# Turning k and q of the second chunk with half-array matmuls in place of quarter ones

## Chip, cores and metric

The kernel runs on one core of a Trainium2 chip. The metric is the device time of one execution in microseconds (us); less is better. All times in this document are in us unless marked ns. The engines of the core have short names: PE is TensorE (its weight loads are listed as PEld), ACT is ScalarE, DVE is VectorE, POOL is GpSimd and SP is SyncE, which issues DMAs.

## What is computed

Attention with a sliding window of 128 positions and 4 sink positions over 4 batches, 8 heads, 768 positions and a head size of 64, followed by a layer norm and an MLP (512 to 2048 to 512) with a residual. Cut to what matters:

```python
scores = scale * np.matmul(q, k.transpose(0, 1, 3, 2))
keep = is_sink | in_window            # pos < 4, or 0 <= i - j < 128
scores = np.where(keep, scores, -1000000000.0)
a = np.exp(scores - max); a = a / (sum + 1e-09)
x = np.matmul(a, v)                   # heads side by side: [4, 768, 512]
xn = (x - mu) / np.sqrt(var + 1e-06) * g_ln
out = x + np.maximum(xn @ w_ch1, 0.0) @ w_ch2
```

## The kernel before

The 3072 rows are worked in 24 tiles of 128 rows; two tiles make a chunk of 256 rows, three chunks a batch. A chunk is loaded, its k and q are turned (transposed, so that the head size lies on the partitions), each of its tiles goes through scores, exponential, masking and the product with v, is centred and transposed (`xnt`), and then the chunk goes through the MLP: eight groups `ph` that write the hidden layer, and after them eight groups `pc` for the output.

Everything is entered as an operation `P.op(name, engines with costs, priority, emit, reads, writes, ...)` in a planner (`Plan`). `Plan.run` places the operations on the engines in simulated time, takes buffers and PSUM banks from rings, picks ACT or DVE where either can do it, and so fixes the order of each engine's program by hand. The `mode` of a PE operation names the tiling of the array (`"q"` quarters, `"c"` column quarters, `"n"` the whole array, `"r"` row halves); where the mode changes the planner adds 0.095. Behind the plan, filler matmuls (L1133) that write an unused bank are put where the plan leaves PE idle for more than 0.3 in the first 24 us.

k and q are turned in three ways. Chunk 0 is cast and turned by whole-array matmuls (L667). Chunks 1, 2 and 3 go through `by_pairs`: one load brings 256 rows as [128 partitions, 8 heads, 2, 64], so that partition p holds the rows 2p and 2p+1 (index i), and matmuls against the identity turn them. From chunk 4 on the DMA engines do it (L691 and L572).

For chunk 1 `by_pairs` is called once for k and once for q (L678), with two PSUM banks of the ring `one` each; for chunks 2 and 3 it is called once for both, with one pair of banks per tensor from the ring `pair`. The turn of a tensor (`tr`, L588) is 32 matmuls (L595), each with 64 rows by 64 columns of the array: 4 head pairs, 2 values of i, 2 heads of the pair (columns of the array) and 2 halves of the partitions (rows, index r). Half r of the partitions holds the rows of tile 2c+r, and its results go to bank r. So each of the two evictions of a tensor (`evict`, L604, run at L638) copies one bank, which is one tile's 128 positions for all head pairs, into `T[:, :, 128 r ...]`. `tile_of[name, tile, half of the heads]` records which eviction a tile's operations have to wait for; here it is the tile's own eviction for both halves of the heads.

`attend_tile` (L723) takes tiles 0 to 3. Its scores run as two operations, j = 0 and 1, with two head pairs each (L748, matmuls L759 for tiles 0 and 1 and L718 in `bands` for tiles 2 and 3); operation j waits for `need[j]` (L728), which is made of `tile_of` entries. For tiles 0 to 2 mask matmuls (`pm`, L739) fill the bank first. `sk` (L771, matmuls L773) makes the scores of the sinks for all head pairs of a tile. `value` (L827) multiplies with v (L840, L845), takes the reciprocal of the sum (L858), scales (L860); `normalise` (L865) takes the statistics (L868, L870), subtracts the mean (L872), and PE transposes the result (L885), which DVE evicts with the gain (L896). The first chunk's MLP groups use L1026, 16 matmuls each; the later chunks use L1033, and the output groups L1062. L1043 and L1045 are the evictions of a `ph` group on ACT and on DVE.

The order of PE around the change is: scores of tiles 0 and 1 (L759) between the turns of k and q of chunk 1 (L595), masks (L739), values of tiles 0 and 1 (L845), scores of tile 2 (L718), transposes of tile 0 (L885), sinks (L773), scores of tiles 2 and 3, then the first `ph` group (L1026) and the transposes of tile 1.

Of the kernel before, what the change touches and what calls it, by code (L numbers as in the profile page):

```python
# [196 lines left out]
def pe(us):  # L197
    return {"PE": (us, us + Plan.PE_DRAIN)}
# [170 lines left out]
def kernel(  # L369
# [12 lines left out]
    nc = tc.nc  # L382
# [19 lines left out]
    P = Plan()  # L402
# [29 lines left out]
    ident_f, ident = const("ident_f", [128, 128], FP32), const("ident", [128, 128], BF16)  # L432
# [21 lines left out]
    Bc = {n: Buf(n) for n in names}  # L454
# [52 lines left out]
    def negs(e):  # L507
# [17 lines left out]
         writes=[Bc["gt"]], dma=HW_T)  # L525
    for h in range(H):
# [3 lines left out]
            reads=[Bc["vc"]], writes=[Bc["vcd"]], nb=3.5 + 0.55 * h)  # L530
    for b in range(B):
# [4 lines left out]
            reads=[Bc["vcd"], Bc["vc"], Bc["sel4" if b else "sel"]], writes=[Bvs[b]], nb=PAR["vs0"][1] if b == 0 else 40.0 * b)  # L536
# [11 lines left out]
    for c in range(4):  # L548
        P.op(f"w2ld{c}", {"POOL": (0.75, 0.8)}, PAR["w2p"][c], lambda e, c=c: G.dma_start(
            w2[c], moe_w_ch2[512 * c:512 * (c + 1), :].rearrange("(t p) n -> p t n", p=128)),  # L550
            writes=[Bw2[c]], dma=SW_W)
# [5 lines left out]
    x_b, xst_b, kT_b, qT_b, vn_b, kts_b = {}, {}, {}, {}, {}, {}  # L557
# [3 lines left out]
    tile_of, scores, trs = {}, {}, {}  # L561
# [11 lines left out]

    def by_pairs(c, what, d):
        b, R = c // RC, c % RC
        nats, pts = [], []
        for nm, src, T, ld in what:
            nat = Buf(f"{nm}n{c}", "natp")
            ap = src[b, :, 256 * R:256 * R + 256, :].rearrange("h (p i) d -> p h (i d)", i=2)
            P.op(f"{nm}ld{c}", {"POOL": (0.9, 0.93)}, ld, lambda e, nat=nat, ap=ap: G.dma_start(  # L580
                nat.t.rearrange("p h i d -> p h (i d)"), ap), writes=[nat], dma=SW_P)
            nats.append(nat)
            pts.append([Buf(f"pt{nm}{c}", "pair")] if len(what) > 1 else [Buf(f"pt{nm}{2 * c + r}", "one") for r in range(2)])

        def half(pt, r):
            return (pt[0].t[:, r, :] if len(pt) == 1 else pt[r].t).rearrange("p (h i m) -> p h i m", h=HP, i=2)

        def tr(e):  # L588
            for nat, pt in zip(nats, pts):
                for hp in range(HP):  # L590
                    for i in range(2):
                        for h2 in range(2):
                            for r in range(2):
                                rs, cs = slice(64 * r, 64 * r + 64), slice(64 * h2, 64 * h2 + 64)
                                nc.tensor.matmul(half(pt, r)[cs, hp, i, :], lhsT=nat.t[rs, 2 * hp + h2, i, :],  # L595
                                                 rhs=ident[rs, rs], start=True, stop=True, skip_group_check=True)
        o = P.op(f"tr{what[0][0]}{c}", pe(0.28 * len(what)), d, tr, reads=nats + [Bc["ident"]], hold=[w[2] for w in what],
                 writes=[x for pt in pts for x in pt], mode="q")
        for (nm, src, T, ld), pt in zip(what, pts):
            for r in range(2):  # L600
                t, done = 2 * c + r, Buf(f"{nm}T{2 * c + r}")
                if c == 1:
                    trs[t] = [o]
                evict(f"ev{nm}{t}", d + 0.05 + 0.02 * r, 512,  # L604
                      lambda pt=pt, r=r: half(pt, r).rearrange("p h i m -> p h m i"),
                      lambda T=T, r=r: T.t[:, :, 128 * r:128 * r + 128].rearrange("p h (m i) -> p h m i", i=2),
                      [pt[-1 if len(pt) == 1 else r]], [T, done], fp=True)
                for hh in range(2):
                    tile_of[nm, t, hh] = done

    def load_v(t, prio):
        b, r = t // RB, t % RB
# [110 lines left out]
    def attend_tile(t):  # L723
        c, i, d = t // 2, t % 2, early(t)
        kT, qT = kT_b[c], qT_b[c]
        own, old = slice(128 * i, 128 * i + 128), slice(128 * (1 - i), 128 * (1 - i) + 128)
        kprev = kT if i else kT_b[0]
        need = [[tile_of[nm, t - o, hh] for nm, o in (("k", 0), ("q", 0), ("k", 1)) if o <= t] for hh in range(2)]  # L728
        ps, pp_s = (Buf(f"ps{t}", "ps"), Buf(f"pss{t}", "one")) if c else (None, None)
        pes = []  # L730
        for j in range(2):
            if t or j == 0:
                pp, pb = Buf(f"s{t}{j}", "pair"), Buf(f"p{t}{j}", "pe")
                pes.append(pb)
                reps, m = (4, neg[:, 0:1]) if t == 0 else (2, neg[:, 1:3] if t == 1 else neg[:, 3:5])

                def mk(e, pp=pp, reps=reps, m=m):
                    for h2 in range(2):
                        nc.tensor.matmul(pp.t[:, h2, :], lhsT=ident,  # L739
                                         rhs=m.rearrange("p b c -> p (b c)").unsqueeze(1).to_broadcast([128, reps, 512 // reps]),  # L740
                                         start=True, stop=False, skip_group_check=True)
                if t < PAR["pm"]:
                    ahead = t + j < 2 and j == 0
                    P.op(f"pm{t}{j}", pe(0.86 if ahead else 0.44), PAR["pm0"] + t if ahead else d + 0.06 + 0.1 * j, mk,
                         reads=[Bc["neg"], Bc["ident"]], writes=[pp], after=[] if ahead else trs[t])
            at_j = slice(0, 512) if t else slice(256 * j, 256 * j + 256)

            def sc(e, pp=pp, j=j):  # L748
                for hp in (2 * j, 2 * j + 1):
                    if t > 1:  # L750
                        col = 256 * (hp % 2)
                        bands(pp, hp, [(kprev, old.start, col, own.start, 64, 128), (kT, own.start, col + 128, own.start, 128, 64)],
                              qT, first=t >= PAR["pm"] and col == 0)
                        continue
                    for n, (kt, ks) in enumerate([(kprev, old), (kT, own)] if t else [(kT, own)]):
                        for h2 in range(2):
                            rs = slice(64 * h2, 64 * h2 + 64)
                            col = 256 * (hp % 2) + 128 * n if t else 128 * hp
                            nc.tensor.matmul(pp.t[:, h2, col:col + 128], lhsT=kt.t[rs, hp, ks], rhs=qT.t[rs, hp, own],  # L759
                                             start=t >= PAR["pm"] and col == 0, stop=True, skip_group_check=True)  # L760
            done = Buf(f"sd{t}{j}")
            P.op(f"sc{t}_{j}", pe(0.2 if t > 1 else 0.25 if t else 0.13), d + 0.1 + 0.1 * j, sc, reads=need[j], **(
                {"rw": [pp], "writes": [done]} if t < PAR["pm"] else {"writes": [pp, done]}),
                 hold=[kT, qT, kprev, pb], mode="q" if t > 1 else "r")
            P.op(f"ex{t}_{j}", {"ACT": act(1024 if t else 512)}, d + 0.11 + 0.1 * j, lambda e, pp=pp, pb=pb, at_j=at_j: nc.scalar.activation(  # L765
                pb.t[:, :, at_j], pp.t[:, :, at_j], AF.Exp, scale=scale), reads=[done], hold=[pp], writes=[pb])
            if t >= PAR["pm"]:
                P.op(f"mk{t}_{j}", {"DVE": dve(1024, 0.52)}, d + 0.12 + 0.1 * j, lambda e, pb=pb: V.tensor_tensor(
                    pb.t, pb.t, mask.rearrange("p a b c -> p a (b c)"), op=ALU.min), reads=[Bc["mask"]], rw=[pb])
        if c:  # L770
            def sk(e):  # L771
                for hp in range(HP):
                    nc.tensor.matmul(pp_s.t[32 * hp:32 * hp + 32, 0:128], lhsT=kts_b[0].t[:, hp, :],  # L773
                                     rhs=qT.t[:, hp, own], start=True, stop=True, skip_group_check=True)
            P.op(f"sk{t}", pe(0.21), d + 0.15, sk, reads=[tile_of["q", t, 0], kts_b[0]], writes=[pp_s], hold=[qT, ps], mode="c")
            P.op(f"sx{t}", {"ACT": act(128)}, d + 0.16, lambda e: nc.scalar.activation(
                ps.t[:, own], pp_s.t[:, 0:128], AF.Exp, scale=scale), reads=[pp_s], writes=[ps])

        def part(h, n):
            return (pes[h // 4 if t else 0].t[:, h % 2, 256 * (h // 2 % 2) + 128 * n:256 * (h // 2 % 2) + 128 * n + 128]  # L780
                    if t else pes[0].t[:, h % 2, 128 * (h // 2):128 * (h // 2) + 128])
        value(c, i, pes, ps, d + 0.3, part, [t - 1, t] if t else [t])
# [307 lines left out]
    for c in range(NC):  # L1090
        mlp(c)
        if c == PAR["x_by_dma"] - 1:
            for s in range(4):
                for j in range(NDM):
                    P.op(f"w1g{s}{j}", {"DVE": fix(0.26)}, 16.0 * c + 11.0 + 2 * s + 0.1 * j,
                         lambda e, s=s, j=j: V.tensor_scalar_mul(w1[s][:, j, :], w1[s][:, j, :], gt[:, j:j + 1]),
                         reads=[Bw1[s], Bc["gt"]], writes=[Bw1g[s]], after=last_use[s])

    def guard(e):
# [8 lines left out]
         reads=[pt_f], writes=[fl_b])  # L1108
# [4 lines left out]
    t = PAR["t0"]  # L1113
    for o in order:
# [6 lines left out]
        if n > 0 and room > 0.3:  # L1121
            free = [(max([e_ for b_, e_ in banks[i].lives if b_ < t], default=0.0), i) for i in range(8)
                    if all(e_ < t or b_ > o.start + 0.3 for b_, e_ in banks[i].lives)]
            if free:
                i = min(free)[1]
# [51 lines left out]
```

## Time and profile before

| | before |
|---|---|
| median of 3 runs | 217.78 (217.46 to 217.9) |
| the profiled execution's own time | 218.01 |
| its span in the profile | 216.5 |
| granted PE clock | 0.999 |
| PE busy | 206.5, 95% of the span, 2781 matmuls in the record |
| turns of chunk 1: L595, bank `one`, 64x64 tiles | 64 matmuls, mean 195 ns of one |
| turns of chunks 2 and 3: L595, bank `pair` | 128 matmuls, mean 194 ns of one |
| evictions of the turned k and q: L638 | 588 to 613 ns on ACT, 683 to 691 ns on DVE |

The mean of one matmul is the time from its start to its modelled end; matmuls overlap, so a group of 32 takes much less than 32 times that. "Idle before" and the name behind the arrow say how long an engine stood idle before an instruction and what released it; "issue" means that nothing which the profile shows was waited for. The chain that ended last is the path from the end of the span back to its start. DMA queues are listed with their packets; q8 and q14 carry instructions.

### The profile page before, as it was taken

How to read it: one execution, taken by the hardware profiler on the slowest of the kernel's cores; microseconds unless marked ns; L12 is line 12 of the kernel's file. 1: busy time of each engine (PE TensorE's matmuls, PEld its weight loads, DVE VectorE, ACT ScalarE, POOL GpSimd, SP SyncE). 2: the span in 40 equal slices, each digit the busy share in tenths (PEclk: the TensorE clock that was granted, in tenths of full speed). 3: DMA queues.
4: the chain of work that ended last, by engine and by line, in shares of the span. 5: the costliest groups of instructions: out<-in, count | busy, mean ns of one | idle time of the engine just before them, and what ended most of it. 6: DMA issues, size and time to landing. Idle time of an engine off the chain costs nothing.

```text
span 216.5 us, 6730 instructions
## 1 busy us (share of the span) xinstructions
PE 206.5 (95%) x2781; PEld 144.7 (67%) x2804; DVE 118.2 (55%) x324; ACT 105.5 (49%) x170; POOL 111.8 (52%) x166
## 2 busy tenths in 40 slices
PE   6898999999999999999999999999999999999993
PEld 2566875765875875874865865864865865865852
DVE  4498874696985447446445446446355355353011
ACT  3885377165572572572562562562562562531610
POOL 7877642499952882871871881871970210210000
PEclk9999999999999999999999999999999999999999
DMA  5999999999999899699999799799999202202103
GB/s 158 171 186 207 194 204 194 178 137 138 185 142 126 155 118 151 84 178 155 101 154 146 115 139 153 111 137 154 120 139 143 78 0 76 73 3 73 48 9 106
DMA packets 103990, 27.82 MB, mean 129 GB/s; under 512 B 94224, under 2 KB 101008, under 8 KB 103952
## 3 DMA queue, kind: packets, MB, share of 16 engines
q0 software_dynamic: 69872, 13.18, 87.0%
q1 hardware_dynamic: 33024, 13.61, 34.4%
q10 hardware_dynamic: 1056, 0.52, 0.9%
q8 instruction: 24, 0.39, 0.8%
q14 instruction: 14, 0.11, 0.2%
HBM read 27.43 MB, written 6.29 MB: 156 GB/s over the span
## 4 chain that ended last, share of the span: by engine, by line
PE 88%; DMA 4%; DVE 4%; issue 2%; SPq 0%; DVEq 0%
PE one L1062 37%; PE one L1033 36%; PE pair L967 3%; DMA natf<-in_k_dram 2%; DMA xnt<-xc 2%; PE one L940 2%; PE one L947 2%; PE one L1026 1%; PE one L956 1%; PE one L975 1%; PE pair L718 1%; PE pair L739 1%; PE one L885 1%; DVE st L868 1%; DVE x L860 1%
## 5 line engine op out<-in xcount | busy, mean ns | idle before, releaser
L1062 PE MATMUL one<-w,h 128*128 128x512 bf16 (+1 forms) x377 | 84.8, 370 | 2.3 <-issue 1.4
L1043 ACT ACTIVATE h<-one 128x512 bf16<-128x512 f32 x93 | 55.6, 598 | 49.6 <-PE one L1033 45.0
L1033 PE MATMUL one<-xnt,w 128*128 128x256 bf16 x704 | 79.3, 273 | 0.0
L1033 PEld LDWEIGHTS <-w 128*128 128x128 bf16 x704 | 68.5, 98 | 10.5 <-DMA xnt<-xc 0.4
L1062 PEld LDWEIGHTS <-h 128*128 128x128 bf16 x400 | 37.2, 98 | 39.1
L985 ACT ACTIVATE pe<-pair 128x768 bf16<-128x768 f32 x36 | 27.2, 808 | 43.0 <-PE pair L967 43.0
L633 POOL DMA_DIRECT2D vn<-in_v_dram x59 | 38.7, 693 | 12.1 <-DMA w<-in_moe_w_ch_dram 6.8
L877 POOL TENSOR_SCALAR st<-st 128x1 f32<-128x1 f32 x24 | 9.1, 378 | 62.2 <-DVE st L870 61.5
L1008 DVE RECIPROCAL rec<-one 128x4 f32<-128x4 f32 x36 | 6.4, 177 | 56.6 <-PE one L956 45.2
L1070 DVE SCALAR_TENSOR_TENSOR ot<-one,st,x 128x512 f32<-128x512 f32 (+1 forms) x25 | 18.2, 727 | 14.1 <-PE one L1062 9.3
L878 POOL TENSOR_TENSOR st<-st,mhalf 128x1 f32<-128x1 f32 x24 | 16.5, 688 | 2.0
L868 DVE BATCH_NORM_STATS2 st<-x 128x6 f32<-128x512 bf16 x24 | 16.7, 694 | 0.8
L1010 DVE TENSOR_TENSOR x<-one,rec 128x256 bf16<-128x256 f32 x36 | 15.3, 424 | 1.2
L691 POOL DMA_DIRECT2D nat<-in_k_dram x16 | 14.9, 938 | 0.9 <-DMA natp<-in_q_dram 0.8
L691 POOL DMA_DIRECT2D nat<-in_q_dram x16 | 14.3, 906 | 0.0
L990 DVE TENSOR_TENSOR pe<-pe,band 128x768 bf16<-128x768 bf16 x24 | 12.2, 550 | 0.0
L872 DVE TENSOR_SCALAR xc<-x,st 128x512 bf16<-128x512 bf16 x24 | 9.0, 375 | 0.9
L967 PE MATMUL pair<-qT,kT 64*64 64x128 bf16 (+1 forms) x528 | 9.2, 204 | 0.0
L1026 PE MATMUL one<-xnt,w 128*128 128x128 bf16 x128 | 8.3, 219 | 0.9 <-issue 0.7
L1026 PEld LDWEIGHTS <-w 128*128 128x128 bf16 x128 | 7.3, 98 | 1.3 <-issue 0.8
L940 PEld LDWEIGHTS <-pe 128*128 128x128 bf16 (+1 forms) x144 | 6.2, 97 | 2.9 <-issue 0.8
L765 ACT ACTIVATE pe<-pair 128x1024 bf16<-128x1024 f32 (+1 forms) x8 | 7.1, 917 | 2.1 <-PE pair L718 1.7
(106 smaller groups left out, 164.6 us busy)
## 6 DMA issues: line engine op xcount, KB each, us to landing
out_dram<-ot SPq DMA_DIRECT2D x23, 256.0 KB
w<-in_moe_w_ch_dram POOLq DMA_DIRECT2D x8, 512.0 KB, 14.7
nat<-in_k_dram POOLq DMA_DIRECT2D x16, 128.0 KB, 4.8
nat<-in_q_dram POOLq DMA_DIRECT2D x16, 128.0 KB, 5.4
vn<-in_v_dram POOLq DMA_DIRECT2D x44, 32.0 KB, 6.0
vn<-in_v_dram POOLq DMA_DIRECT2D x15, 64.0 KB, 5.5
natp<-in_k_dram POOLq DMA_DIRECT2D x3, 256.0 KB
vn<-in_v_dram POOLq DMA_DIRECT2D x6, 128.0 KB, 11.0
```

The costliest lines, as they stand in the source:

```text
L633: P.op(f"vld{t}_{i}", {"POOL": (0.8, 0.85)}, prio + 0.001 * i, lambda e, p0=p0, n=n, hs=hs, src=src: G.dma_start(m.t[p0:p0 + n, hs, 0:64], ...
L691: lambda e, nat=nat, ap=ap: G.dma_start(nat.t, ap), writes=[nat], dma=SW, after=gate(c))
L868: P.op(f"bn{t}", {"DVE": fix(0.60)}, d + 0.12, lambda e: V.bn_stats(st.t[:, 8:14], x.t), reads=[x], writes=[st, mv])
L878: G.tensor_tensor(st.t[:, 16:17], st.t[:, 17:18], mhalf, op=ALU.pow)),
L967: nc.tensor.matmul(pps[u].t[64 * g:64 * g + 64, h2, col + c0:col + c0 + n], lhsT=kt.t[rs, hp, k0:k0 + 64], rhs=qT.t[rs, hp, q0:q0 + n], st ...
L985: nc.scalar.activation(pes[j].t.rearrange("p a b -> p (a b)")[:, 0:768].rearrange("p (a b) -> p a b", a=2), pps[j].t[:, :, 0:384], AF.Exp, ...
L1010: P.op(f"x{t - 1}{u}", {"DVE": dve(256)}, d + 0.051 + 0.002 * u, lambda e, u=u, rc=rc, pv=pv: V.tensor_tensor(x.t[:, 256 * u:256 * u + 256 ...
L1026: nc.tensor.matmul(ph.t[:, 128 * s:128 * s + 128], lhsT=w1[u // 2][:, j, 128 * s:128 * s + 128], rhs=xnt.t[:, j, 128 * (u % 2):128 * (u % ...
L1033: nc.tensor.matmul(ph.t[:, 256 * s:256 * s + 256], lhsT=w1[ht // 4][:, j, 128 * (ht % 4):128 * (ht % 4 + 1)], rhs=xnt.t[:, j, :], start=j ...
L1043: nc.scalar.activation(hb.t, ph.t, AF.Relu)
L1062: nc.tensor.matmul(pc.t[:, 0:wd], lhsT=(h1[2 * s + i].t[:, 128 * ii:128 * ii + 128] if by_tile else h1[ht // 2].t[:, 256 * (ht % 2) + 128 ...
L1070: V.scalar_tensor_tensor(ot.t[:, sl], in0=pc.t[:, 0:wd], scalar=st.t[:, 16:17], in1=x.t[:, sl], op0=ALU.mult, op1=ALU.add),
```

## The change

`by_pairs` gets a second way, `whole`, used when it is called for one tensor alone, that is for chunk 1. There the turn of a tensor is 16 matmuls with all 128 rows and 64 columns of the array: 4 head pairs, 2 values of i, 2 heads. The moving operand is the whole identity (128 columns instead of 64). Head pairs 0 and 1 go to the first bank, 2 and 3 to the second, with all 256 positions of the chunk. So the first eviction of a tensor now copies two head pairs of both tiles, and the second the other two. `tile_of` is changed to match: both tiles' score operation j waits for the evictions j of k and q. `sk`, which needs all head pairs, waits for both evictions of q. The planner is told 0.45 instead of 0.28 for a turn, and a mode `"h"`. Chunks 2 and 3 keep the quarter matmuls.

```diff
-        nats, pts = [], []
+        nats, pts, whole = [], [], len(what) == 1
...
                     for i in range(2):
+                        for h2 in range(2) if whole else ():
+                            nc.tensor.matmul(pt[hp // 2].t[64 * h2:64 * h2 + 64, 256 * (hp % 2) + 128 * i:256 * (hp % 2) + 128 * i + 128],
+                                             lhsT=nat.t[:, 2 * hp + h2, i, :], rhs=ident, start=True, stop=True, skip_group_check=True)
+                        if whole:
+                            continue
                         for h2 in range(2):
                             for r in range(2):
...
-        o = P.op(f"tr{what[0][0]}{c}", pe(0.28 * len(what)), d, tr, reads=nats + [Bc["ident"]], hold=[w[2] for w in what],
-                 writes=[x for pt in pts for x in pt], mode="q")
+        o = P.op(f"tr{what[0][0]}{c}", pe(0.45 if whole else 0.28 * len(what)), d, tr, reads=nats + [Bc["ident"]], hold=[w[2] for w in what],
+                 writes=[x for pt in pts for x in pt], mode="h" if whole else "q")
...
                 evict(f"ev{nm}{t}", d + 0.05 + 0.02 * r, 512,
-                      lambda pt=pt, r=r: half(pt, r).rearrange("p h i m -> p h m i"),
-                      lambda T=T, r=r: T.t[:, :, 128 * r:128 * r + 128].rearrange("p h (m i) -> p h m i", i=2),
+                      lambda pt=pt, r=r: pt[r].t.rearrange("p (h i m) -> p h m i", h=2, i=2) if whole else
+                      half(pt, r).rearrange("p h i m -> p h m i"),
+                      lambda T=T, r=r: (T.t[:, 2 * r:2 * r + 2, :] if whole else T.t[:, :, 128 * r:128 * r + 128]
+                                        ).rearrange("p h (m i) -> p h m i", i=2),
                       [pt[-1 if len(pt) == 1 else r]], [T, done], fp=True)
                 for hh in range(2):
-                    tile_of[nm, t, hh] = done
+                    tile_of[(nm, 2 * c + hh, r) if whole else (nm, t, hh)] = done
...
-            P.op(f"sk{t}", pe(0.21), d + 0.15, sk, reads=[tile_of["q", t, 0], kts_b[0]], writes=[pp_s], hold=[qT, ps], mode="c")
+            P.op(f"sk{t}", pe(0.21), d + 0.15, sk, reads=[tile_of["q", t, 0], tile_of["q", t, 1], kts_b[0]], writes=[pp_s], hold=[qT, ps], mode="c")
```

## Prediction

> **What bounds the kernel now.** I read the page first: busy time, then the chain that ended last.
>
> ```profile
> span 216.5 us, 6730 instructions
> ...
> PE 206.5 (95%) x2781; PEld 144.7 (67%) x2804; DVE 118.2 (55%) x324; ACT 105.5 (49%) x170; POOL 111.8 (52%) x166
> ...
> q8 instruction: 24, 0.39, 0.8%
> ...
> PE 88%; DMA 4%; DVE 4%; issue 2%; SPq 0%; DVEq 0%
> ```
>
> TensorE (PE) is busy 95% of the span and is 88% of the chain. A change in the first 25 us counts only if it moves the moment from which PE never stops again. Next, the timeline of PE and then of VectorE (DVE) around the change (start, length, [idle before <- releaser]):
>
> ```profile
> 9.95 0.44 PE L595 MATMUL one<-ident,natp 64*64 64x64 bf16 x32
> 10.39 0.59 PE L739 MATMUL pair<-neg,ident 128*128 128x512 bf16 x2
> ...
> 11.51 0.51 PE L1133 MATMUL pair<-const-bfloat16-1.0 128*128 128x256 bf16 x3
> 11.94 0.44 PE L595 MATMUL one<-ident,natp 64*64 64x64 bf16 x32
> ...
> 15.41 0.84 PE L1026 MATMUL one<-xnt,w 128*128 128x128 bf16 x12
> 16.98 0.38 PE L1026 MATMUL one<-xnt,w 128*128 128x128 bf16 x4 [0.73 <-issue]
> ...
> 25.64 0.40 PE L885 MATMUL one<-ident,xc 128*128 128x128 bf16 x4 [0.36 <-DVE xc L872]
> ```
>
> ```profile
> 10.45 0.69 DVE L638 CAST kT<-one 128x512 bf16<-128x512 f32 x1 [0.34 <-PE one L595]
> 11.15 0.18 DVE L858 RECIPROCAL rec<-one 128x4 f32<-128x4 f32 x1
> ...
> 16.45 0.58 DVE L872 TENSOR_SCALAR xc<-x,st 128x512 bf16<-128x512 bf16 x1
> 17.40 0.69 DVE L1045 TENSOR_SCALAR h<-one 128x512 bf16<-128x512 f32 x1 [0.37 <-PE one L1026]
> 18.01 0.68 DVE L896 TENSOR_TENSOR xnt<-one,gt 128x512 bf16<-128x512 bf16 x1
> ```
>
> The last long idle of PE before the steady stretch ends at 25.64, where tile 3's transposes (L885) wait for its centred x (L872). That comes out of DVE, which works back to back from 10.45, when the k turn of the second chunk is done, to 25.59. It has two holes: 0.37 at 17.40 and 0.09 at 23.61. So the end moves with DVE's row of work, and the change touches its start (the k turn) and, less plainly, the 0.37.
>
> The 0.37 comes from PE: the first MLP group (L1026, 16 matmuls) stops for 0.73 after its 12th, with "issue" as releaser: no semaphore, no data. The 13th begins at instruction 449 of PE's program. Queue q8 "instruction" carries 24 packets, 0.39 MB: 16 KB each. The first starts at 14.48 and takes 0.94; from it to the 22nd PE's program advances by 5165 instructions, 246 a packet. I read the pause as PE at the edge of its loaded code, waiting for the first refill, with a boundary at instruction 449 and one about 246 to 256 earlier, near 193 to 203.
>
> **The Trainium skill on this pause.** Its page "Runtime: NRT & Kernel Launch", section "Instruction fetch mechanics", says that code is refilled in blocks of 16 KiB (256 instructions), the next fetched while the current one runs, so that crossing a boundary is mostly hidden. The packet size agrees; the 0.73 is not hidden. By that rule the pause would be something else and stay where it is, which is the second rival below.
>
> **The change, part by part.**
>
> *Removed and added on PE.* Per tensor, 32 quarter matmuls become 16 half matmuls; PE's program loses 32 instructions (weight loads count) for k and 32 for q. Quarters start four within 10 ns, groups 32 ns apart; the last of k starts at 10.201 and ends at 10.394, 0.445 after the first (9.949). Halves stream 128 columns. The trace has no 128x64 tile. Nearest are L759 (64x128 tiles, 128 columns): two start 3 ns apart, pairs 53 to 63 ns apart; and L773 (128x32 tiles): four start within 10 ns, so column tiles run side by side. I take pairs at 63 once, then 53.5 six times: last start 0.384, plus 0.219 (a 128-column matmul) = 0.603. **Cost per turn +0.16 us.** Low end: nothing, were a pair to pass in a quarter group's 32 ns; high end, no overlap: 15 steps of 53 to 56 ns, plus 0.219, about 1.03, so +0.59. I take the middle value since L759 streams the same 128 columns in the same pairs.
>
> *k's turn.* DVE's eviction of k now takes the second bank, finished last: 10.45 becomes 10.61. DVE has no slack up to 17.03, so the centred x of tile 1 (L872) ends at 17.19. On PE, the mask matmuls (L739) at 10.39 were waiting for ScalarE's exponential, so PE itself slips only 0.07.
>
> *q's turn.* It costs PE 0.16 again, but one filler matmul (L1133) of 0.114 ahead of it is gone, so PE is at +0.08 behind it. Its evictions are ScalarE's, which is in an exponential from 11.61 to 12.63 and takes them back to back; the cover is that exponential, and without it 0.16 would be due. The sink scores (L773, 14.06) now wait for both q evictions: the second ended at 13.60 and ends by about 13.7, so nothing; queued behind them on PE are the masks of L739 and the scores of tiles 2 and 3, which would be as late as they. Transposes of tile 0 (L885, 13.73) wait for DVE, so from there PE is at +0.16.
>
> *The first MLP group.* 66 fewer instructions lie ahead (64 and the filler's two). Instruction 449 is now in tile 3's scores (L718, at 18.3 before) instead of in the group. The group runs 15.57 to about 16.7 without the pause. If the refill is asked for at instruction 193, that is reached some 0.7 later (12.2 for 11.5), and the code is there at 16.98 + 0.7 = 17.7, still ahead of 18.3. Price of this edit: between 0 and -0.73 on PE.
>
> *What DVE gets of it.* L1045 starts at 17.19 instead of 17.40: the hole of 0.37 goes, the 0.16 is paid. L896 behind it needs tile 1's transposes, which start when the centred x is there (17.24, was 17.20) and end at 17.6, before 17.8. From there DVE is at **+0.158 - 0.373 = -0.215**.
>
> *The planner's move.* The program's order shows one more difference: the fourth MLP group (16 matmuls, 0.90) goes ahead of tile 3's first value matmuls, with one filler (0.114) behind those. Those value matmuls would start near 22.2 and end at 22.65; the DVE reciprocal that reads them comes at 22.68. Nothing, or 0.05; its low end is -0.05 from the 0.09 hole. From the fifth group on, PE's order is the same.
>
> *Where it lands.* Tile 3's transposes start at 25.42, and the MLP groups behind them follow without a gap. Weights cap the gain: software DMA is 99% busy there. The second block of w2 lands at 33.09 and is used at 33.55, so no more than about 0.4 can be passed on. At -0.215 all landings stay ahead.
>
> Sum: span 216.5 - 0.215 = 216.3. The profiled execution took 218.01, 0.23 above the median of 217.78, with 1.5 outside its span that nothing touches. On the median: **217.57**.
>
> **Rivals.**
>
> *Slower: the halves do not run side by side.* Place: each turn; price +0.59 for k on DVE. q's turn then sets tile 2's scores, tile 0's transposes and the xnt eviction (L896, 14.23, +0.82), so the centred x of tile 1 ends at 17.85 and L1045 starts 0.45 late: 218.23. It decides from pairs 89 ns apart on: the extension 6c - 0.163 then eats the 0.37 hole. For it: no 128x64 tile has been seen, and weights now come from all 128 rows. Against: L759, L773 and the quarters overlap, along rows, along columns and both.
>
> *The pause stays with the 13th matmul.* Then the hole stays and everything is 0.16 late: 217.94. For it: the refill packet had ended at 15.42, 1.56 before the pause did, which I can't explain. Against: no semaphore, no data and no other such pause in the span.
>
> *More gain.* If the 0.09 hole also closes, and L872 at 16.45 takes 0.35, as at 13.32 and 25.23, instead of 0.58 (GpSimd starts a load beside it), up to the cap of 0.4: 217.38.
>
> *It doesn't do what it says.* The program's order shows the 16 halves and the shorter code, so only the size is open.
>
> **How the numbers follow.** Forecast 0.50, more gain 0.15, pause stays 0.17, no overlap 0.18. From no change this measurement tells about 0.2%, 0.44 us (the runs shown spread over that): faster means below 217.34, slower above 218.22. Faster 0.24: two thirds of "more gain" and the lower quarter of the forecast's spread. Slower 0.14: half of "no overlap" and a little of "pause stays". Same 0.62. The range reaches from below the cap's 217.38 to "no overlap", with some of the runs' spread: 217.15 to 218.25.
>
> **What would show it.** In the profile after: the k turn 0.55 to 0.65 long with pairs about 54 ns apart; the group at 15.4 to 15.6 whole, without "issue" inside; L1045 straight behind L872; tile 3's L885 near 25.4. Wrong if the pause turns up elsewhere on PE before 25, if pairs are nearer 100 ns apart, or if PE gains a wait for weights around 31 to 34.

## The result, and the profile after

| | before | after |
|---|---|---|
| median on the chip of the result, 17 runs each | 217.78 (217.27 to 218.76) | 218.68 (217.58 to 219.17) |
| ratio, after to before | | 1.0029 [1.0015, 1.0043] |
| the profiled execution's own time | 218.01 | 217.82 |
| its span | 216.5 | 216.3 |

The forecast was 217.57, with a range of 217.15 to 218.25. The profile, one execution of each kernel, did what was forecast (a span shorter by 0.2); the median did not: it rose by 0.90. The rest of this document is about that contradiction.

From the page of the changed kernel (span; busy time by engine; the code queue; the chain that ended last):

```profile
span 216.3 us, 6688 instructions
...
PE 208.9 (97%) x2772; PEld 145.0 (67%) x2772; DVE 118.4 (55%) x324; ACT 105.6 (49%) x170; POOL 111.0 (51%) x166
...
q8 instruction: 23, 0.38, 0.8%
...
PE 88%; DVE 5%; DMA 4%; POOL 1%; issue 1%; DVEq 0%
```

Its lines lie 7 higher from L608 on (L872 is L879, L1026 is L1033, L1045 is L1052); L595 became L600, and the half matmuls are L593. The timelines of PE, of VectorE (DVE) and of GpSimd (POOL) in the same stretch as before (start, length, [idle before <- releaser]):

```profile
9.21 0.64 PE L593 MATMUL one<-ident,natp 128*64 128x128 bf16 x16
11.57 0.64 PE L593 MATMUL one<-ident,natp 128*64 128x128 bf16 x16 [0.27 <-DMA natp<-in_q_dram]
...
15.30 1.07 PE L1033 MATMUL one<-xnt,w 128*128 128x128 bf16 x16
16.90 0.40 PE L892 MATMUL one<-ident,xc 128*128 128x128 bf16 x4 [0.54 <-DVE xc L879]
...
25.36 0.40 PE L892 MATMUL one<-ident,xc 128*128 128x128 bf16 x4 [0.58 <-DVE xc L879]
```

```profile
9.89 0.69 DVE L645 CAST kT<-one 128x512 bf16<-128x512 f32 x1 [0.70 <-PE one L593]
...
16.30 0.54 DVE L879 TENSOR_SCALAR xc<-x,st 128x512 bf16<-128x512 bf16 x1
16.77 0.67 DVE L1052 TENSOR_SCALAR h<-one 128x512 bf16<-128x512 f32 x1
...
20.18 0.55 DVE L879 TENSOR_SCALAR xc<-x,st 128x512 bf16<-128x512 bf16 x1
...
22.53 0.18 DVE L865 RECIPROCAL rec<-one 128x4 f32<-128x4 f32 x1
22.99 0.42 DVE L867 TENSOR_TENSOR x<-one,rec 128x256 bf16<-128x256 f32 x1 [0.28 <-DVE rec L865]
```

```profile
19.80 0.83 POOL L549 DMA_DIRECT2D w<-in_moe_w_ch_dram  x1 [0.60 <-DMA w<-in_moe_w_ch_dram]
```

The reader is to see four things. The first MLP group (L1033 at 15.30) runs whole, without its "issue" pause, and L1052 stands right behind L879: the hole of 0.37 is gone. The turns came 0.74 earlier than before (9.21 for 9.95) because the first loads landed earlier in this execution, and half of that was given back to q's load (q's turn at 11.57 for 11.94), so the two front ends can't be compared by their clock times alone. The centring of tile 2 (L879 at 20.18) takes 0.55; it ends at 20.73, 0.09 behind the end of GpSimd's issue of a weight load (19.80 + 0.83 = 20.63). And there is a new hole of 0.28 between tile 3's reciprocal and the scaling that follows it.

### The profile page after: what moved, and what is told of

It is laid out like the page before. It is cut to its first block, busy times and chain, and to the rows that moved or that the text cites. A ratio compares the mean times of both kernels' runs of the same rounds, so it can differ in the third digit from the quotient of the medians.

```text
span 216.3 us, 6688 instructions
## 1 busy us (share of the span) xinstructions
PE 208.9 (97%) x2772; PEld 145.0 (67%) x2772; DVE 118.4 (55%) x324; ACT 105.6 (49%) x170; POOL 111.0 (51%) x166
## 4 chain that ended last, share of the span: by engine, by line
PE 88%; DVE 5%; DMA 4%; POOL 1%; issue 1%; DVEq 0%
PE one L1069 39%; PE one L1040 36%; DMA natp<-in_q_dram 4%; PE pair L974 3%; PE one L947 2%; PE one L954 2%; PE one L963 1%; DVE st L875 1%; DVE xnt L903 1%; PE one L982 1%; PE one L1033 1%; DVE xc L879 1%; DVE x L867 1%; PE pair L600 1%; PE pair L725 1%
## 5 line engine op out<-in xcount | busy, mean ns | idle before, releaser
L1069 PE MATMUL one<-w,h 128*128 128x512 bf16 (+1 forms) x400 | 87.7, 371 | 0.0
L1040 PEld LDWEIGHTS <-w 128*128 128x128 bf16 x704 | 68.6, 98 | 10.3
L884 POOL TENSOR_SCALAR st<-st 128x1 f32<-128x1 f32 x24 | 8.5, 352 | 61.7 <-DVE st L877 61.1
L885 POOL TENSOR_TENSOR st<-st,mhalf 128x1 f32<-128x1 f32 x24 | 16.3, 678 | 2.0
L879 DVE TENSOR_SCALAR xc<-x,st 128x512 bf16<-128x512 bf16 x24 | 8.9, 369 | 0.9
L1033 PE MATMUL one<-xnt,w 128*128 128x128 bf16 x128 | 8.2, 219 | 0.0
L974 PEld LDWEIGHTS <-kT 64*64 64x64 bf16 x528 | 7.2, 108 | 0.4 <-issue 0.4
```

Source lines behind the costliest of these rows:

```text
L885: G.tensor_tensor(st.t[:, 16:17], st.t[:, 17:18], mhalf, op=ALU.pow)),
L974: nc.tensor.matmul(pps[u].t[64 * g:64 * g + 64, h2, col + c0:col + c0 + n], lhsT=kt.t[rs, hp, k0:k0 + 64], rhs=qT.t[rs, hp, q0:q0 + n], st ...
L1040: nc.tensor.matmul(ph.t[:, 256 * s:256 * s + 256], lhsT=w1[ht // 4][:, j, 128 * (ht % 4):128 * (ht % 4 + 1)], rhs=xnt.t[:, j, :], start=j ...
L1069: nc.tensor.matmul(pc.t[:, 0:wd], lhsT=(h1[2 * s + i].t[:, 128 * ii:128 * ii + 128] if by_tile else h1[ht // 2].t[:, 256 * (ht % 2) + 128 ...
```

## The experiments

All were timed beside the kernel before on the same chip. Its median was 218.56, 218.47, 217.82, 217.88 and 218.42 on the five chips of the experiments, which are counted here from first to fifth, apart from the chip of the result. Three theories at first: P, the refill pause of PE comes at another place or depends on the length of the program; O, the planner's other order costs it; H, the half matmuls' longer turns cost it.

**The changed kernel again** (no edit).

> The changed kernel once more, for its spread and for a second profile. Its 17 times fall into two groups, 217.6 to 218.3 (7) and 218.5 to 219.2 (10); the profiled execution is of the first group. Theory P (a pause for code that comes in some executions at another place than before): a profile of the second group shows an idle stretch of 0.5 to 1.0 us on PE with 'issue' as releaser. Theory O (the planner's new order of the fourth MLP group) and theory H (the halves' longer turns): a second-group profile shows no such pause; the time is lost by DVE or by waits for weights between 9 and 35 us. Ratio to before 1.002 to 1.005 under all.

218.92 (217.85 to 219.84, 12 runs), ratio 1.0001 [0.9973, 1.0029]. In this execution k's turn began at 9.96, as in the profile before (9.95), so the steps can be set side by side. PE and DVE of this run:

```profile
20.49 0.35 DVE L879 TENSOR_SCALAR xc<-x,st 128x512 bf16<-128x512 bf16 x1
```

```profile
25.46 0.40 PE L892 MATMUL one<-ident,xc 128*128 128x128 bf16 x4 [0.56 <-DVE xc L879]
```

k's eviction starts at 10.64 (before 10.45), tile 1's centring ends at 17.16 (17.03), L1052 starts at 17.08 (17.40), tile 3's transposes at 25.46 (25.64), the last output at 212.79 (213.01). The path is 0.18 to 0.22 shorter, as forecast, and the times show none of it.

**Quarters in the new order.** The planner is told the new cost and mode, the matmuls stay quarters.

```diff
-        o = P.op(f"tr{what[0][0]}{c}", pe(0.28 * len(what)), ...
+        o = P.op(f"tr{what[0][0]}{c}", pe(0.45 if len(what) == 1 else 0.28 * len(what)), ...
-                 ..., mode="q")
+                 ..., mode="h" if len(what) == 1 else "q")
```

> Quarter matmuls as before, but the planner is told the new cost and mode, so that the order and the fillers are those of the changed kernel. Theory P: program as long as before up to 2 instructions, so the time of before, within 0.1%. Theory O: slow as the changed kernel, 1.002 to 1.005. Theory H: the time of before.

219.53 (217.64 to 220.79, 12), ratio 1.0036 [1.0004, 1.0067]. The pause is there (0.47, at the same instruction). Tile 3's centring took twice its 0.35; DVE and GpSimd:

```profile
25.28 0.69 DVE L872 TENSOR_SCALAR xc<-x,st 128x512 bf16<-128x512 bf16 x1
```

```profile
25.00 0.87 POOL L615 DMA_DIRECT2D vn<-in_v_dram  x1 [1.62 <-DMA w<-in_moe_w_ch_dram]
```

It ends at 25.97, again 0.09 behind the end of a GpSimd issue (25.88). And the last packet of the last store came 2.7 behind its issue, more than 1.1 later than in the other profiles so far.

**Halves in the old order.**

```diff
-        o = P.op(..., pe(0.45 if whole else 0.28 * len(what)), ... mode="h" if whole else "q")
+        o = P.op(..., pe(0.28 * len(what)), ... mode="q")
```

> Half matmuls, but the planner is told the old cost and mode, so that the order and the fillers are those of before. Theory P: slow as the changed kernel, 1.002 to 1.005, since the program is 64 instructions shorter. Theory O: the time of before, or 0.1% less. Theory H: slow as the changed kernel.

218.55 (217.31 to 219.48, 12), ratio 1.0 [0.9972, 1.0029]. No pause in the front. Tile 3's transposes at 25.36, but PE waits 0.17 for a DMA transpose near 103 (0.16 in the profile of this kernel on the fourth chip, none in that on the second), and the last output came at 213.02.

**Halves, program as long as before.** Behind each half matmul the same one with a single column: 16 matmuls, 32 instructions, in each turn (the expectation says 32 matmuls).

```diff
+                            nc.tensor.matmul(pt[hp // 2].t[64 * h2:64 * h2 + 64, 256 * (hp % 2) + 128 * i:256 * (hp % 2) + 128 * i + 1],
+                                             lhsT=nat.t[:, 2 * hp + h2, i, :], rhs=ident[:, 0:1], start=True, stop=True, skip_group_check=True)
```

> The changed kernel with 32 more one-column matmuls in each of the two turns (each repeats the first column of the matmul before it), so that the program is as long as before. Theory P: the first MLP group pauses again for about 0.7 us as before, and the time is that of before plus 0.1 to 0.2 us. Theories O and H: slow as the changed kernel or slower, 1.002 to 1.006.

218.76 (217.74 to 219.46, 12), ratio 1.002 [0.9992, 1.0048]. The pause did not come back with the length: the code packet started at 13.95, earlier than in the profile before (14.48), and PE never waited for it. In the other profiles of the halves it started at 15.47 or later. So the length puts the boundary; that an early packet is why it was not felt here fits, but rests on this one profile.

On this chip the changed kernel is level with the kernel before, so the times decide between none of the three theories. No profile of the changed kernel shows a pause at another place so far, which speaks against P.

**Second chip: changed, before, halves in the old order, quarters in the new order**, unchanged from above; "before" under another name measures what two rows of one kernel differ by.

> The changed kernel once more, for the times of more executions and one more profile. Theory M (the change shortens the profiled path by 0.2 us, and what moves the median is how many executions end with a late last store, a late first load or a slow centring of tile 3, up to 1.2 us together, which falls on every kernel alike): the ratio to the kernel before lies within 0.997 to 1.003 and within the same distance of 1 as that of the kernel before sent under another name; in the profile the third tile's centred transposes begin 15.5 to 15.6 us after the turn of k where q's load is not waited for, and from there to the last output is 187.3 to 187.4. Theory C (the change itself costs 0.3% of the median, as on the first chip): ratio 1.002 to 1.005, with the kernel before under another name at 0.999 to 1.001. Theory O (the planner's order costs it, not the half matmuls): this one and the quarters in the new order at 1.002 to 1.005, the halves in the old order at 0.998 to 1.001.

> The kernel before under another name, a measure of what two rows of executions of one kernel on one chip differ by. Theory M: ratio within 0.997 to 1.003, its interval about 0.005 wide, times in two groups some 1.2 us apart. Theories C and O: 0.999 to 1.001. In the profile the refill pause of TensorE in the front is there (0.5 to 0.75 us, after its 449th instruction).

> Half matmuls with the planner's cost and mode of the kernel before, so its order. Theory M: 0.997 to 1.003; in the profile no refill pause in the front, the third tile's x 0.20 us after its reciprocal, the path to the third tile's centred transposes shorter by 0.2 to 0.3 us than that of the kernel before from the same start. Theory C with its cause in the half matmuls: 1.002 to 1.005. Theory O: 0.998 to 1.001.

> Quarter matmuls in the order that the planner makes for the halves. It was 1.0036 [1.0004, 1.0067] on the first look, and its profile had a slow centring of tile 3 (0.69 for 0.35 us) and one completion packet of the last store 1 us after the other 15. Theory M: both were luck and are mostly gone, ratio 0.997 to 1.003. Theory O: 1.002 to 1.005 again, with tile 3's centring again at 0.69. Under both the pause of TensorE after its 449th instruction is there (0.45 to 0.75), and tile 3's x comes 0.45 after its reciprocal.

Ratios: changed 1.0007 [0.9981, 1.0032], before 1.0 [0.9976, 1.0025], halves in the old order 1.0003 [0.9974, 1.0032], quarters in the new order 1.0001 [0.9977, 1.0025]. All times of these four lie within 217.3 to 219.3. In the quarters in the new order the pause that was expected did not come; the first MLP group was whole, behind a wait of 0.66 for its weight block. Two readings of the profiles count. In the old order (here the halves) tile 3's scaling follows its reciprocal at once, as in the kernel before (0.03 in all nine profiles of that order); DVE:

```profile
22.76 0.17 DVE L865 RECIPROCAL rec<-one 128x4 f32<-128x4 f32 x1
22.96 0.42 DVE L867 TENSOR_TENSOR x<-one,rec 128x256 bf16<-128x256 f32 x1
```

And in the kernel before, PE lost time ahead of the first MLP group in another way than the pause:

```profile
16.17 1.07 PE L1026 MATMUL one<-xnt,w 128*128 128x128 bf16 x16 [0.63 <-DMA w<-in_moe_w_ch_dram]
```

Here the group is whole too, but it starts late because the first weight block landed late, near 16.1 (14.91 in the first profile of before).

**Third chip: two copies of each kernel.**

> Two copies of the changed kernel and two of the kernel before, on one chip, to tell a lasting difference from luck, and for four more profiles. Ratios so far: 1.0029 on the first chip, 1.0001 and 1.0007 on two others; the means of the changed kernel were 0.68, 0.13 and 0.10 us above those of the kernel before. Theory M (the path of the first 25 us is shorter by 0.1 to 0.2 us, and what an execution adds at its ends, the first loads and the last store, hides it): the two copies of the changed kernel lie on both sides of the two of the kernel before, or within 0.2% of them, and in the four profiles the transposes of tile 3 begin in the changed kernel 0.1 to 0.2 us sooner on average. Theory C (the change costs 0.1 to 0.3% on every chip): both copies of the changed kernel 1.001 to 1.004, both of the kernel before 0.999 to 1.001. A profile of a longer execution (218.6 us or more) shows what makes it long: under M a late end of the last store (over 3.7 us from the last output's computing to the end of the span) or tile 3's centring at 0.69 us, with the 187.3 us between the same as ever; under C a wait between 25 and 213 us that the shorter ones do not have.

> As for the first copy of the changed kernel: ratio 0.999 to 1.001 under theory C, 0.997 to 1.003 under theory M; in the profile the pause of TensorE after its 449th instruction (0.45 to 0.75 us), and 187.3 us from tile 3's transposes to the last output.

> As for the first copy of the changed kernel: 1.001 to 1.004 under theory C; under theory M its ratio differs from that of the first copy by as much as from that of the kernel before, up to 0.3%. No pause of TensorE after its 449th instruction.

> As for the other copy of the kernel before: ratio 0.999 to 1.001 under theory C, 0.997 to 1.003 under theory M; the pause of TensorE after its 449th instruction is in the profile.

Changed 1.0019 [1.0003, 1.0034] and 1.0015 [0.9998, 1.0032]; before 1.0003 [0.9991, 1.0014] and 1.0003 [0.999, 1.0016]. That is theory C by the times (the change costs something on every chip), and theory M by the profiles (its path is shorter, and what an execution adds at its ends hides that): the second copy of before was caught in a long execution (219.01), and all of its length was at the end, 4.49 from the last output's start to the end of the span (3.3 to 3.4 in the other three).

**Fourth chip: is it the race for tile 3's centring?** In the changed kernel's profiles that centring starts within 0.05 of GpSimd's issue of a v load in four of five, in those of before 0.16 to 0.27 ahead of it. So that load was moved, in both kernels, behind tile 3's variance:

```diff
-            writes=[bv], dma=SW, after=list(ones_of.values()))
+            writes=[bv], dma=SW, after=list(ones_of.values()) + ([rs_op[3]] if t == 5 else []))
```

> The changed kernel with one v load (tile 5's, issued by GpSimd near 25.0 to 25.3 us) moved behind tile 3's variance on GpSimd, so that it cannot be issued beside tile 3's centring on VectorE; nothing else moves. Theory R (race): the changed kernel loses 0.33 us or more in the executions in which that issue comes first, and this one never does: 0.2 to 0.4 us faster than the changed kernel in this call on average, ratio to the kernel before 0.998 to 1.000; in the profile tile 3's centring takes 0.35 and the v load is issued after 26 us. Theory T (luck at both ends of an execution, first loads and last store): no difference from the changed kernel beyond 0.1 us, ratio as for that one. Theory V (the later v load is missed by tile 5's value matmuls): slower than the changed kernel, with a wait of TensorE for v between 27 and 45 us.

> The kernel before with the same v load moved. Theory R: its centring of tile 3 comes 0.16 to 0.32 us ahead of the issue in the profiles, so it seldom loses: ratio 0.9985 to 1.0005. Theory T: 1.000 within its interval. Theory V: slower by as much as the changed kernel with the load moved is slower than the changed kernel.

> The changed kernel as it is, for the comparison on one chip. Theories R and C: ratio 1.0005 to 1.003 with single times spread between 217.3 and 219.3; theory T: 0.998 to 1.002.

> The half matmuls in the order of the kernel before, so without the move of tile 3's value matmuls; in its two profiles the centring came 0.50 and 0.65 us ahead of the issue. Theory R: no lost race, and the front's gain of about 0.1 us: ratio 0.998 to 1.0005, 0.1 to 0.4 us below the changed kernel. Theory T: no difference from the changed kernel beyond 0.1 us.

Changed with the load moved 1.0025 [0.9999, 1.005], before with it moved 1.0028 [1.0002, 1.0055], changed 1.0021 [0.9996, 1.0047], halves in the old order 1.0005 [0.9979, 1.003]. Theory R (the race) falls: without the race the changed kernel is no shorter (218.69 for 218.61). The kernel before with the load moved is a warning: its mean lies 0.54 above that of the kernel before (standard error 0.22), more than the changed kernel's 0.40 (0.18), though its path is as long as ever (187.3 from tile 3's transposes to the last output). So rows of the same path can differ by as much as the change seems to cost. But all four profiles were of long executions, 218.80 to 218.99, and all show where the length is. In one the first loads were late (k's turn at 10.94). In the other three it is the end: 4.50 to 4.60 behind the last output's start. The DMA view from 212.5 to 217.5 (40 slices of 0.125; busy tenths, GB/s), first the changed kernel on this chip, then that of the first profile; both issue the last store at 213.2:

```profile
DMA  0028971000100001988201100060000000000000
GB/s 0 0 74 287 344 246 33 0 8 8 8 0 16 16 8 41 336 311 295 66 16 25 74 16 0 0 131 0 0 0 0 0 0 0 0 0 0 0 0 0
```

```profile
DMA  0029871010000189820300004000000000000000
GB/s 0 0 98 319 311 238 25 8 8 0 16 16 8 57 311 352 271 58 0 131 0 0 0 0 131 0 0 0 0 0 0 0 0 0 0 0 0 0 0 0
```

The burst near 213 is the store before the last, the one from 214.4 (214.1 in the second row) the last. In the second row it is over at 214.75. In the first it trails: a trickle of 16 to 74 GB/s until 215.5. The trace's records of single packets say what trickles: in five profiles of long executions (of before, before with the load moved, changed, halves and quarters alike) the last packets of that store start 2.3 to 2.7 behind its issue, one behind the other, and in the thirteen other profiles up to here they start 1.35 to 1.62 behind it. The issue itself takes SyncE longer too, 0.68 to 0.95 in the five and 0.33 to 0.58 in the thirteen. And in each of the five, a 16 KB packet of the code queue had ended late: 0.31 to 0.58 behind the store's issue, having taken 1.20 to 1.46; in the thirteen it ended between 0.07 ahead and 0.27 behind, having taken 0.88 to 1.10. It starts 0.6 to 0.95 ahead of the store, when PE has done its last matmuls and jumps over the fallback code behind the plan.

**Fifth chip: no jump at the end.** The fallback (for rows whose sums are out of range, which these inputs do not have) and the branch over it are left out of both kernels.

```diff
-    bad = nc.values_load(flag, min_val=0, max_val=128 * NT * H)
-    with tc.If(bad > 0):
...
-        general(tc, nc, slots, pairs, ones, ident_f, ident, w1, w2, mhalf, g_s, g_r, q, k, v, out, scale)
```

> The kernel before without the jump at its end: the fallback for rows whose sums are out of range, and the branch over it, are left out (the rows that it would mend do not occur in these inputs), so that no engine needs new code at the end. Theory T (the packet that brings TensorE the code behind the jump makes the last store late in the executions of the longer group): no 16 KB code packet in the last 4 us of the profile, times in one group no wider than 0.8 us but for single late first loads, median 0.8 to 2 us below that of the kernel before. If the groups come from elsewhere: two groups 1 us apart as ever. Under both: 187.3 us from tile 3's transposes to the last output.

> The changed kernel without the fallback and the branch over it, the same edit. If the 0.35 us lies in the end of the execution, in how often the jump's code packet collides with the last store: this kernel and the kernel before with the same edit within 0.1 us of each other, or this one up to 0.2 us shorter. If it lies in the front (the planner's order of tile 3's value matmuls, 0.08 + 0.07 us in the profiles, and what GpSimd's issues add to tile 2's and tile 3's centring): this one 0.15 to 0.4 us longer than the kernel before with the same edit.

| 12 runs each | median | range | mean, standard deviation | ratio to the kernel before |
|---|---|---|---|---|
| before, no jump | 217.58 | 217.25 to 217.88 | 217.59, 0.19 | 0.9966 [0.9944, 0.9987] |
| changed, no jump | 217.49 | 217.34 to 218.10 | 217.59, 0.23 | 0.996 [0.9941, 0.998] |

The kernel before itself ran at 218.42 (217.25 to 219.33) beside them, with a standard deviation of 0.68. Without the jump the spread falls to a third, the long executions are gone, and the two kernels do not differ. The edit takes out three things together: the reading of the flag, the branch on the engines, and the code behind it. So it shows that the long ends come with these three; that PE's code packet is the one that makes them is read from the timing in the traces above. The DMA view of before without the jump, same window: the store's burst ends at once and nothing follows.

```profile
DMA  1899200000299710000000000000000000000000
GB/s 41 287 328 328 66 0 0 0 0 0 90 328 360 246 25 0 0 0 0 0 0 0 0 0 0 0 0 0 0 0 0 0 0 0 0 0 0 0 0 0
```

The changed kernel's profile on this chip shows one thing more, in PE's timeline:

```profile
17.37 0.28 PE L725 MATMUL pair<-qT,kT 64*64 64x64 bf16 x7
17.80 0.28 PE L725 MATMUL pair<-qT,kT 64*64 64x64 bf16 x9 [0.15 <-issue]
```

The front ran early (tile 1's centring ended at 16.28), the code packet started at 15.50 and ended at 16.40, and PE stopped in tile 3's scores ahead of its 224th matmul. In the profile before it stopped ahead of its 224th matmul as well, in the first MLP group.

## Where the time went

The means of starts in all profiles of the two kernels with the jump and the fallback in place and the first loads not late (the five of before include the one with the v load moved, which changes nothing up to there; six of the changed kernel):

| | L1045 or L1052 | tile 2's centring ends | tile 3's reciprocal | tile 3's transposes | last output |
|---|---|---|---|---|---|
| before | 17.27 | 21.03 | 22.75 | 25.49 | 212.83 |
| changed | 16.90 | 20.86 | 22.67 | 25.48 | 212.83 |
| changed, less | 0.36 | 0.17 | 0.08 | 0.01 | 0.00 |

The gain is real at the first column and is spent in three places. 0.19 goes to tile 2's centring: DVE comes earlier and meets GpSimd's issue of a weight load, which waits for an earlier weight block to land and so moves less than DVE (its mean start is 19.93 for 20.07, the centring's 20.31 for 20.63). In five of the six profiles the centring then takes 0.54 to 0.66 and ends 0.09 behind the issue's end; in before it is 0.35 to 0.50, as here in the first profile:

```profile
20.77 0.41 DVE L872 TENSOR_SCALAR xc<-x,st 128x512 bf16<-128x512 bf16 x1
```

Then 0.09 goes to tile 3's reciprocal and 0.06 to what stands behind it: the planner's move puts the value matmuls of tile 3 behind an MLP group. These two steps hardly vary between executions: the reciprocal starts 1.81 behind that centring's end (1.71 or 1.72 in before), and the transposes 2.81 to 2.83 behind the reciprocal (2.74 or 2.75). From tile 3's transposes to the last output it is 187.3 or 187.4 in both.

The times seem to hold a second effect. On the chip of the result and the first four of the experiments the changed kernel's mean lies 0.68, 0.13, 0.10, 0.33 and 0.40 above that of before (weighted by their errors 0.35, standard error 0.07), and that difference is gone with the jump (0.00 on the fifth chip, standard error 0.09). The 0.07 takes every execution as independent, which flatters it: the kernel before with the load moved lay 0.54 above, and the quarters in the new order 0.79 on one chip and 0.14 on another, while before under other names lay between 0.04 below and 0.18 above. Taken as real, the difference lies in the end, in how often and how far the last store is late. Why that would happen more often in the changed kernel was not found: the packet starts 0.06 earlier ahead of the store than in before (0.91 to 0.94 for 0.85 to 0.88, one profile 0.61), but so it does in the halves in the old order, which were within 0.0005 of before on three chips, and it does not in the quarters in the new order, which were 1.0036 on one. That stays open.

## Why the prediction was wrong, step by step

- *The cost of a turn*, +0.16: right in kind, a little small. The turn takes 0.637 for 0.444, and from the same start the eviction of k came 0.19 later. The two matmuls of a pair start 3 or 4 ns apart, and the next pair starts 52 or 53 ns behind the second of them (77 once). The rival "do not run side by side" is out.
- *The pause*: right in where the boundary goes (tile 3's scores, seen in the last run), and the first group is whole in every profile of the changed kernel. The kernel before shows the pause in two of its six profiles with quarters and in three a late weight block instead, 0.56 to 0.79; one, without the jump, has neither. The code packet starts before that block lands in before (13.7 to 14.5; 15.47 or later in the changed kernel). That it delays the block is not shown: behind packets at 14.03 to 14.28 the block came near 16.1 to 16.3 in four profiles of quarters, but in five others with packets at 13.71 to 14.49 (one of them the padded halves) it landed at 14.91 to 15.31.
- *What DVE gets of it*, -0.215: from the same start it came out at -0.18 at tile 3's transposes, which is in part luck. There L1052 came 0.32 earlier, not 0.215 (it starts 0.08 ahead of the centring's end, which a sum over holes leaves out), the planner's move took about 0.15 of it back, and this was the one profile of six in which GpSimd did not hold tile 2's centring. Averaged over executions the forecast does not hold, because the profiled execution of before was a late one at its front, and because the sum let everything behind L1045 move along with DVE. The prediction saw GpSimd beside L872 at 16.45, but only as a chance of more gain; that an earlier DVE would run into the next issue was missed.
- *The planner's move*, "nothing, or 0.05": this step failed. It costs 0.15. The prediction compared the end of the moved matmuls with the reciprocal's start (22.65 and 22.68) and so left 0.03 between them. In all eleven profiles of the new order, halves or quarters, the reciprocal waits for them and starts 0.105 to 0.107 behind the modelled end of the first half's; in the old order they had ended 0.64 or more ahead of it. The scaling then starts 0.27 or 0.28 behind the reciprocal (0.03 in the old order), within 0.02 of the end of the second half's matmuls. What holds it stays open: the trace lists no wait for PE there, only for the reciprocal itself, and in the old order the scaling runs while those matmuls run.
- *On the median*, "with 1.5 outside its span that nothing touches": this is the step that put the forecast on the wrong side. What lies outside the span is indeed 1.45 to 1.66 in all runs with the jump, but the last 3.3 to 4.6 inside it, from the last output on, differ by more than 1 between executions of one kernel, and the sum took them as fixed. The gain, 0.2, is a fifth of that. In the result ten of the changed kernel's 17 executions took more than 218.5 and three of those of before; why so many more is open.
- *The rivals on the slower side* (no overlap of the halves, a pause that stays) named the wrong mechanisms; neither was seen. The chance of "faster" is 0.225 by the terms given for it, not 0.24.

The Trainium skill, page "SBUF — State Buffer", section "SBUF: two separate sides", says that a VectorE operation in a two-port mode and a GpSimd operation exclude each other for a whole instruction. The traces agree for the centring where it starts well inside a DMA issue of GpSimd: in the first 27 us of the twenty profiles, 29 centrings that started 0.26 or more behind the issue's start were held until 0.09 to 0.11 behind its end. They do not where it starts early in the issue: ten that started up to 0.17 behind the issue's start took their 0.35 and were not held. Whether the centring runs in a two-port mode no trace here shows. The page "Runtime: NRT & Kernel Launch", section "Instruction fetch mechanics", calls the crossing of a code block mostly hidden. Here the first crossing was not felt in sixteen of the twenty profiles and cost PE 0.15 to 0.73 in four.

## What to carry to other kernels

A sum made on one profile says what a path gains; before it is carried to the median, look at how much the first loads and the last store differ between executions, and where that is more than the gain, forecast no change with a skewed range. When an engine is made earlier, look down its row for the next operation that shares something with an engine that is not made earlier. A branch at the end of a program is paid for: leaving it out, with the fallback behind it, made this kernel 0.84 faster at the median on one chip (217.58 for 218.42) and its times three times as steady, more than the change could have brought, at the price of a kernel without its fallback.

## What was not expected of the hardware

- A code packet of 16 KB takes 0.88 to 2.10 (median 1.03 over all profiles), and where PE paused it went on only 1.4 to 1.6 after the packet's end (15.42 to 16.98, 15.16 to 16.73, 15.43 to 16.99 and 16.40 to 17.80 in four profiles).
- Where such a packet ended 0.31 or more behind the issue of the last store, the store's last packets were about 1 late (five profiles of eighteen), though the code queue holds 0.8% of the DMA engines' time. That the packet is the cause is argued from the timing.
- DVE's centring of 128x512 takes 0.35 alone and 0.36 to 0.81 when it starts well inside a DMA issue of GpSimd, even where GpSimd computes nothing.
